# Early Strassen blocks: weight splits and conversion moved into second-layer steps, and two tiles of the last plain chunk put between the first block's halves

## The chip, the cores and the metric

The kernel runs as one program on one core of one Trainium2 chip. The metric is the device time of that core in microseconds (us). Most executions of a kernel agree within 0.3%.

## The reference, cut to what matters

Attention over 2 batches, 8 heads, 576 tokens of 64 values gives `x` (1152 tokens by 512). Two feed-forward stages follow:

```
p = domain_probs / (domain_probs.sum(-1, keepdims=True) + 1e-09)
for e in range(E):                       # E = 4, w1[e]: 512 x 1024, w2[e]: 1024 x 512
    h = np.maximum(x @ w1[e], 0.0)
    out += p[:, e:e + 1] * (h @ w2[e])
...
h = x @ w_in                             # 512 x 2048
g = h * (1.0 / (1.0 + np.exp(-1.702 * h)))
return (g @ w_out)                       # 2048 x 512
```

All of it is wanted in fp32. The kernel makes each fp32 product out of three products of rounded parts: every operand is split into a rounded part (`hi`, made by ScalarE) and the rest (`lo`, raw minus `hi`, made by VectorE), and hi*hi + lo*hi + hi*lo are added up in PSUM.

## The kernel before, in words

The hidden layers are cut into 12 blocks of 512 hidden units (8 of the first stage, numbers 0 to 7, and 4 of the second). A `visit` is one block with a list of chunks of tokens; its first layer (512 inputs to 512 hidden units) has one step per group `g` of 128 hidden units, and its second layer one step per tile of 128 tokens, 12 matrix products of 128x512 each (line 972). The first-layer weights of a visit are called "a", those of the second layer "b"; each comes as four pieces g = 0 to 3, loaded in pairs into four buffers `wst` by SyncE's queue, and each piece is split by `split_w`: ScalarE writes `whi` (line 60), and VectorE `wlo` (line 230) when `rest` is run, one step later.

Visits 0 to 6 are plain: their chunks run while attention is still going on. Visit 6 ends with chunk 3, tokens 768 to 1151, which is three tiles in its second layer. Visits 7, 8 and 9 (blocks 3, 1 and 0) are the first three that compute the first layer by Strassen's scheme over two chunks of 320 tokens; this text calls them **block 1, block 2 and block 3**, and visit 10 **block 4**. Each of blocks 1 to 3 has

- a first half and a second half (kind 3, 7 steps each, one product of 6 matrix instructions per step, line 885). In the listings a product is known by its operands: `xh` or `th` are tokens and sums of tokens, `whi` is a weight and `sh` a sum of weights. A half begins with xh,whi and ends with xh,sh, which adds the last product to the bank `pc`;
- the second layer (kind 4, 8 steps on five banks: the first five tiles with half of the hidden units, and then three of them with the other half), and
- two steps left over (kind 5), which run between the halves of the next block.

Around the products, each half has a chain of small work on the 320-column banks: ScalarE copies the bank of the first product to `u` (line 909); VectorE adds the second product to it (line 930), makes a second sum (line 914), and writes `jc` (line 891, three times), of which the first must have read the bank `pc` before the last product may be added there. ScalarE applies relu (line 893) and rounds to `hh`, GpSimd makes `hl` (line 895). The remaining quarter goes through lines 962 and 963.

The sums of weights are made by GpSimd (`sr`, lines 251 to 254) and split by `split_sums` into `sh` (ScalarE, two instructions) and `sl` (VectorE, line 267, two). There is one buffer each for `sh` and `sl`, so a half's sums are written after the half before has read its own. `evac_l2` (line 1005, or 1003 for the first visit of a tile) adds a finished tile of the second layer to the result.

Where the splits stand is written out by hand in `place()` for visits 7 to 9, and the order of the instructions of VectorE, ScalarE, GpSimd and TensorE in these visits is fixed as the code issues them (`pin_turn`). What is issued for visit 6 is not fixed so: the scheduler puts it where it likes. Each engine works through its own queue in order.

`mlp_convert` runs beside all this: the second stage's weights arrive as 8-byte numbers and each of 32 pieces is turned into fp32 by one ScalarE and six VectorE instructions (lines 342 to 357), one `yield` at a time; `cv_due` says how many per step. The pieces are stored to DRAM and loaded again into `wst` when their block comes.

Of the kernel before, what the change touches and what calls it, by code (L numbers as in the profile page):

```python
# [21 lines left out]
NCH = len(CH)  # L22
# [3 lines left out]
OVER = 2  # L26
# [8 lines left out]
NMOE = 8  # L35
# [4 lines left out]
def attn_moe_mlp(ctx: ExitStack, tc: tile.TileContext, qk0, qk1, qk2, v0, vp, fg, dp, wa_moe, wb_moe, wa_mlp, wb_mlp, out):  # L40
# [115 lines left out]
    for p_, u in zip(units[1:], units[2:]):  # L156
        seq += [(1,) + u, (2,) + p_]
    seq.append((2,) + units[-1])
    before = []
    for v_ in range(v_exp, len(visits)):  # L160
        b, cs = visits[v_]
        if v_ == v_mlp:
# [16 lines left out]
    w_turn = [("a", 0), ("b", 0)]  # L179
    for u in seq:  # L180
        if u[1] + 1 < len(visits) and u in (last_l1[u[1]], last_l2[u[1]]):
            w_turn.append(("ab"[u[0] in (2, 4, 5)], u[1] + 1))
    w_pairs = [(k, v_, g) for k, v_ in w_turn for g in (0, 2)]
    w_loaded = [0]
    w_owed = [0]
# [939 lines left out]
        return rest  # L1125

    def steps(kind, v_, b, c):
        return {1: 4, 2: len(tiles(c)), 3: 7, 4: 10 - OVER, 5: OVER}[kind]

    split_q = []  # L1130

# [12 lines left out]
    def place():  # L1144

        at = {}

        def put(u, g, what, *args):
            at.setdefault((u, g), []).append((what, args))

        for v_ in range(v_exp, v_all):
            b, (c1, c2) = visits[v_]
            h0, h1, l2 = (3, v_, b, c1), (3, v_, b, c2), (4, v_, b, c1)
            put(h0, 1, sum_weights, v_ + 1, 0)
            put(h1, 1, sum_weights, v_ + 1, 1)
            put(l2, 0, split_sums, v_ + 1, 0)
            put((5, v_, b, c1), 0, split_sums, v_ + 1, 1)
            first = v_ == v_exp
            places = [(h1, 1), (h1, 3), (l2, 1), (l2, 2)]
            for g, (u, i) in enumerate(places):  # L1160
                put(u, i, split_w, "a", v_ + 1, g)
            if first:
                for k, (u, i) in enumerate([(h0, 2), (h0, 4), (h1, 4), (h1, 6)]):
                    put(u, i, split_w, "b", v_, k)
            for k, i in enumerate((3, 4, 6, 7) if first else (3, 4, 5, 6)):
                put(l2, i, split_w, "b", v_ + 1, k)
        return at

    place_at = place()
    evac = [lambda: None]  # L1170
# [3 lines left out]
    for i, (kind, v_, b, c) in enumerate(seq):  # L1174
# [17 lines left out]
            j_gen = emit_joint(v_, b, m)  # L1192
        n_steps = steps(kind, v_, b, c)
        for g in range(n_steps):
            if kind in (2, 4, 5):
                split_until("b", v_, range(4))
            else:
                split_until("a", v_, [g] if kind == 1 else range(4))
            if i == 0:
                ev = lambda: None  # L1200
            elif kind == 3:
                ev = next(j_gen)
            else:
                ev = {1: emit_l1, 2: emit_l2, 4: emit_l2_joint}[kind](v_, b, c, g) if kind < 5 else emit_l2_joint(v_, b, c, g, True)
            for _ in range(sums_at.get(u, 0)):
                in_turn(next, ts_gen, None)
            if sum_due:
                sv, sm = sum_due[0][:2]
                if (sv, 0) in j_done if sm else sv - 1 not in joint or (sv - 1, 1) in j_done:
                    split_sums()  # L1210
            if kind == 3 and g == 6:
                j_done.add((v_, m))
            n = 0
            if nxt:
                j, cc = nxt[0]
                left = sum(steps(*u) for u in seq[i:j]) - g
                n = max(0, -(-(due[cc] - pulled[0]) // left))
                for _ in range(n):
                    pull()
            rests = []  # L1220
            for d in split_due[:]:
                d[0] -= 1
                if d[0] == 0:
                    split_due.remove(d)
                    rests.append(split_output(d[1]))
            evac[0]()
            for r in rests:
                r()
            evac[0] = ev
            split_next()  # L1230
            if len(split_q) > 4:
                split_next()
            for what, args in place_at.get((u, g), ()):
                what(*args)
            if v_ + 1 < len(visits) and not v_exp <= v_ < v_all:
                if u == last_l1[v_] and kind == 1:
                    split_q.append(("a", v_ + 1, g))
                elif u == last_l1[v_] and g in (3, 5):
                    split_q.append(("a", v_ + 1, g // 4))
                if u == last_l2[v_] and g == n_steps - 1 and v_ + 1 != v_exp:  # L1240
                    split_q.extend(("b", v_ + 1, k) for k in range(4))
            if late:

                if sums_at.get(u, 0) < 2:
                    cv_due[0] += (0.25 if v_ < v_all else 1.55 if b < NMOE else 1.3) * (4 / n_steps)
                while cv_due[0] >= 1:
                    in_turn(next, cv_gen[0], None)
                    cv_due[0] -= 1
                load_owed()
            if v_ >= v_exp:  # L1250
                (pin_engines.add if v_ < v_all else pin_engines.discard)(nc.tensor.engine)
                pin_turn()
            else:
                pin_from[1] = len(nc.cur_bb.bb.instructions)
# [58 lines left out]
```

## Time and profile before

| | |
|---|---|
| median of 3 runs | 708.8 us (706.63 to 709.87) |
| profiled execution: time | 709.05 us |
| its span, first to last instruction | 707.3 us |
| mean granted TensorE clock | 0.995 |
| busy share of the span | TensorE 97%, VectorE 72%, ScalarE 48%, GpSimd 32% |

The span is read against the time of its own execution, 1.75 us more. TensorE's share says that only some 19 us of the span can be won without taking work from it; where these lie is what the views below are for. In the timeline a row `x2` is two instructions merged, its start is the first's start, and `[1.61 <-ACT sh L60]` is the time that the engine stood idle before it and the instruction that ended the wait. The chain of work that ended last is followed back from the last instruction.

### The profile page before, as it was taken

How to read it: one execution, taken by the hardware profiler on the slowest of the kernel's cores; microseconds unless marked ns; L12 is line 12 of the kernel's file. 1: busy time of each engine (PE TensorE's matmuls, PEld its weight loads, DVE VectorE, ACT ScalarE, POOL GpSimd, SP SyncE). 2: the span in 40 equal slices, each digit the busy share in tenths (PEclk: the TensorE clock that was granted, in tenths of full speed). 3: DMA queues.
4: the chain of work that ended last, by engine and by line, in shares of the span. 5: the costliest groups of instructions: out<-in, count | busy, mean ns of one | idle time of the engine just before them, and what ended most of it. 6: DMA issues, size and time to landing. Idle time of an engine off the chain costs nothing.

```text
span 707.3 us, 10721 instructions
## 1 busy us (share of the span) xinstructions
PE 688.6 (97%) x3829; PEld 598.4 (85%) x3829; DVE 510.6 (72%) x1057; ACT 341.8 (48%) x789; POOL 225.0 (32%) x266
## 2 busy tenths in 40 slices
PE   8999999999999799899999999999999999999997
PEld 4797888888898687888888888887899898998986
DVE  6896766676386668685868977887888878675632
ACT  5777766676432734443443343335355455352430
POOL 6887566622223535411412314112102212000000
PEclk9999999999999899999999999999999999999999
DMA  7686744432310333232324424424320444120012
GB/s 266 225 283 234 268 146 159 126 100 82 118 31 31 90 90 109 84 134 86 98 101 150 145 94 136 155 92 144 115 104 31 130 138 150 60 76 0 1 45 89
DMA packets 38597, 83.37 MB, mean 118 GB/s; under 512 B 3560, under 2 KB 3568, under 8 KB 38544
## 3 DMA queue, kind: packets, MB, share of 16 engines
q1 hardware_dynamic: 38504, 82.65, 35.6%
q8 instruction: 30, 0.49, 0.3%
q14 instruction: 23, 0.19, 0.1%
q10 hardware_dynamic: 40, 0.04, 0.0%
HBM read 71.88 MB, written 10.78 MB: 117 GB/s over the span
## 4 chain that ended last, share of the span: by engine, by line
PE 81%; DVE 11%; ACT 3%; issue 2%; POOL 1%; DMA 1%; SPq 0%; DVEq 0%; POOLq 0%; ACTq 0%
PE m L972 36%; PE m L847 19%; PE m L885 14%; PE s L568 4%; PE x L672 4%; PE t L642 3%; DVE wlo L230 2%; DVE hl L963 1%; DVE acc L1005 1%; DVE sl L267 1%; DVE cvd L355 1%; DVE wf L357 1%; DVE jc L891 1%; ACT jc L893 1%; ACT hh L60 1%
## 5 line engine op out<-in xcount | busy, mean ns | idle before, releaser
L972 PE MATMUL m<-whi,hh 128*128 128x512 f32 x432 | 123.2, 395 | 0.2
L972 PE MATMUL m<-wlo,hh 128*128 128x512 f32 x432 | 119.9, 392 | 0.0
L972 PE MATMUL m<-whi,hl 128*128 128x512 f32 x432 | 119.3, 391 | 0.0
L230 DVE TENSOR_TENSOR wlo<-wst,whi 128x512 fp32r<-128x512 f32 x140 | 109.7, 800 | 5.3 <-ACT whi L60 4.7
L972 PEld LDWEIGHTS m<-wlo,hh 128*128 128x128 f32 x432 | 81.5, 189 | 17.3
L972 PEld LDWEIGHTS m<-whi,hl 128*128 128x128 f32 x432 | 81.2, 189 | 17.0
L895 POOL TENSOR_TENSOR hl<-jc,hh 128x320 fp32r<-128x320 f32 x42 | 37.4, 892 | 178.1 <-ACT hh L60 168.1
L60 ACT ACTIVATE whi<-wst 128x512 fp32r<-128x512 f32 x144 | 85.0, 625 | 15.7 <-DMA wst<-in_wa_moe_dram 7.0
L972 PEld LDWEIGHTS m<-whi,hh 128*128 128x128 f32 x432 | 79.7, 189 | 14.6 <-DVE acc L1005 0.8
L893 ACT ACTIVATE jc<-jc 128x320 f32<-128x320 f32 x42 | 19.7, 470 | 111.3 <-DVE jc L891 111.3
L251 POOL TENSOR_TENSOR sr<-wst 128x256 f32<-128x256 f32 x20 | 18.7, 936 | 147.1 <-DVE tl L287 49.1
L624 POOL TENSOR_SCALAR e<-e,sm 128x128 f32<-128x128 f32 (+4 forms) x72 | 47.6, 672 | 54.4 <-DVE sm L622 28.1
L847 PE MATMUL m<-xh,whi 128*128 128x256 f32 (+2 forms) x304 | 64.2, 328 | 0.0
L847 PE MATMUL m<-xh,wlo 128*128 128x256 f32 (+2 forms) x304 | 64.2, 325 | 0.0
L847 PE MATMUL m<-xl,whi 128*128 128x256 f32 (+2 forms) x304 | 63.8, 326 | 0.0
L963 DVE SCALAR_TENSOR_TENSOR hl<-m,hh 128x384 fp32r<-128x384 f32 (+2 forms) x82 | 36.0, 439 | 27.9 <-ACT hh L962 27.5
L1005 DVE SCALAR_TENSOR_TENSOR acc<-m,dpn,acc 128x512 f32<-128x512 f32 x63 | 46.8, 746 | 12.7 <-PE m L972 12.6
L847 PEld LDWEIGHTS m<-xh,whi 128*128 128x128 f32 x304 | 50.3, 189 | 3.7 <-DVE acc L1005 0.5
L847 PEld LDWEIGHTS m<-xh,wlo 128*128 128x128 f32 x304 | 50.6, 189 | 2.6
L847 PEld LDWEIGHTS m<-xl,whi 128*128 128x128 f32 x304 | 50.3, 189 | 2.8
L966 DVE TENSOR_TENSOR hl<-m,hh 128x384 fp32r<-128x384 f32 x48 | 26.7, 556 | 29.0 <-ACT hh L60 28.9
L614 ACT ACTIVATE e<-e,mx 128x128 f32<-128x128 f32 (+4 forms) x72 | 41.6, 580 | 11.7 <-DVE mx L598 11.2
(138 smaller groups left out, 1296.6 us busy)
## 6 DMA issues: line engine op xcount, KB each, us to landing
wst<-in_wa_moe_dram SPq DMA_DIRECT2D x28, 512.0 KB, 3.6
wst<-in_wb_moe_dram SPq DMA_DIRECT2D x28, 512.0 KB, 4.3
mst<-in_wa_mlp_dram SPq DMA_DIRECT2D x16, 512.0 KB, 3.8
wm<-wf SPq DMA_DIRECT2D x32, 256.0 KB, 3.3
mst<-in_wb_mlp_dram SPq DMA_DIRECT2D x16, 512.0 KB, 4.1
wst<-wm SPq DMA_DIRECT2D x16, 512.0 KB, 3.7
cb<-cumd SPq DMA_DIRECT2D x16, 256.0 KB, 3.9
qr<-in_qk_dram SPq DMA_DIRECT2D x8, 384.0 KB, 4.8
```

The source lines that it names most:

```text
L60: return nc.scalar.activation(out=out, in_=in_, func=AF.Copy)
L230: (nc.gpsimd if v_ == 0 and kind == 'a' and g < 4 else nc.vector).tensor_sub(lf, raw, f(hf))
L568: nc.tensor.matmul(pt[:, :z - a], lhsT=lr[i][0], rhs=lr[i][1], start=i == 0 and not (both and pt is not bank), stop=i == n - 1, skip_group ...
L614: nc.scalar.activation(out=e[:, off:off + w], in_=e[:, off:off + w], func=AF.Exp, scale=-1.0, bias=mx, accum_out=sm[:, 0, k:k + 1])
L624: nc.gpsimd.tensor_scalar(out=e[:, off:off + w], in0=e[:, off:off + w], scalar1=sm[:, 0, i:i + 1], scalar2=1.0, op0=ALU.mult, op1=ALU.mult)
L672: nc.tensor.matmul(pt[64 * g:64 * g + 64, o:n], lhsT=lhsT, rhs=rhs, start=i == 0, stop=i == nk - 1)
L847: nc.tensor.matmul(p[:, :n], lhsT=w[:, k, :], rhs=x[c][:, k, :], start=(j == 0 and k == 0), stop=(j == 2 and k == 3))
L885: nc.tensor.matmul(p[:, :WN], lhsT=w[a][:, k, :], rhs=x[z][:, k, :], start=start and j == 0 and k == 0, stop=stop and j == 2 and k == 1, s ...
L895: nc.gpsimd.tensor_sub(hl[:, g, :], r, f(hh[:, g, :]))
L963: nc.vector.scalar_tensor_tensor(out=l_, in0=q, scalar=0.0, in1=f(h_), op0=ALU.max, op1=ALU.subtract)
L972: nc.tensor.matmul(p, lhsT=h_tile(v_, b, c, j, x, k), rhs=wb[v_, k][w].rearrange("p a c -> p (a c)"), start=i == 0 and k == 0, stop=i == 2 ...
L1005: nc.vector.scalar_tensor_tensor(out=a, in0=p, scalar=d, in1=a, op0=ALU.mult, op1=ALU.add)
```

## The change

Four things, in one diff. (1) The second layer of visit 6's last chunk keeps one step; its last two tiles become a kind of their own, 6, issued between the halves of block 1, and the split of the sums for block 1's second half is put behind the first of them. (2) In blocks 1 to 3 the splits leave the early steps of the second half (steps 1 and 3; in block 1 also 2 and 4 of the first half and 4 of the second) for steps 5 and 6 of the second half and 1 to 6 of the second layer; block 1, which also splits its own "b", has two more at each end (steps 0 and 1 of its first half, and of block 2's). (3) The second layer no longer wants all of "b" split at its start; the rests are run when the half that needs them begins. (4) The conversion gets 0.75 of a step's share in the second-layer steps of blocks 1 to 3 and none in their products (0.25 in all before), and 1.4 in place of 1.55 later.

```diff
-    before = []
+    before = [(6,) + units[-1]]
...
-            w_turn.append(("ab"[u[0] in (2, 4, 5)], u[1] + 1))
+            w_turn.append(("ab"[u[0] not in (1, 3)], u[1] + 1))
...
     def steps(kind, v_, b, c):
-        return {1: 4, 2: len(tiles(c)), 3: 7, 4: 10 - OVER, 5: OVER}[kind]
+        if (kind, v_) == (2, v_exp - 1) and c == NCH - 1:
+            return len(tiles(c)) - OVER
+        return {1: 4, 2: len(tiles(c)), 3: 7, 4: 10 - OVER, 5: OVER, 6: OVER}[kind]
...
             first = v_ == v_exp
-            places = [(h1, 1), (h1, 3), (l2, 1), (l2, 2)]
-            for g, (u, i) in enumerate(places):
-                put(u, i, split_w, "a", v_ + 1, g)
+            places = [(h1, 5), (h1, 6)] + [(l2, i) for i in range(1, 7)]
             if first:
-                for k, (u, i) in enumerate([(h0, 2), (h0, 4), (h1, 4), (h1, 6)]):
-                    put(u, i, split_w, "b", v_, k)
-            for k, i in enumerate((3, 4, 6, 7) if first else (3, 4, 5, 6)):
-                put(l2, i, split_w, "b", v_ + 1, k)
+                put((6,) + units[-1], 0, split_sums_done)
+                nxt0 = (3, v_ + 1, visits[v_ + 1][0], c1)
+                places = [(h0, 0), (h0, 1)] + places + [(nxt0, 0), (nxt0, 1)]
+            todo = [("b", v_)] * first + [("a", v_ + 1), ("b", v_ + 1)]
+            for (kind, w_, g), (u, i) in zip([(*t, g) for t in todo for g in range(4)], places):
+                put(u, i, split_w, kind, w_, g)
         return at
+
+    def split_sums_done():
+        if sum_due:
+            sv, sm = sum_due[0][:2]
+            if (sv, 0) in j_done if sm else sv - 1 not in joint or (sv - 1, 1) in j_done:
+                split_sums()
...
-            if kind in (2, 4, 5):
+            if kind in (2, 6):
                 split_until("b", v_, range(4))
-            else:
+            elif kind not in (4, 5):
                 split_until("a", v_, [g] if kind == 1 else range(4))
...
-                ev = {1: emit_l1, 2: emit_l2, 4: emit_l2_joint}[kind](v_, b, c, g) if kind < 5 else emit_l2_joint(v_, b, c, g, True)
+                if kind in (4, 5) and ("b", v_, 2 if kind == 5 or g > 4 else 0) in lo_of:
+                    split_rest()
+                ev = (emit_l1(v_, b, c, g) if kind == 1 else emit_l2(v_, b, c, g) if kind == 2 else
+                      emit_l2(v_, b, c, g + len(tiles(c)) - OVER) if kind == 6 else emit_l2_joint(v_, b, c, g, kind == 5))
...
-                    cv_due[0] += (0.25 if v_ < v_all else 1.55 if b < NMOE else 1.3) * (4 / n_steps)
+                    cv_due[0] += ((0.75 if kind == 4 else 0) if v_ < v_all else 1.4 if b < NMOE else 1.3) * (4 / n_steps)
```

Both programs hold the same instructions on every engine; only their order differs. TensorE first, in the middle of block 1's first half after the change (line 972 is one of the two tiles of visit 6, line 885 a product; the last row is the half's last product's first pair):

```order
L885 MATMUL m<-tl,sh 128x320 x2
L972 MATMUL m<-whi,hh 128x512 x4
L972 MATMUL m<-wlo,hh 128x512 x4
L972 MATMUL m<-whi,hl 128x512 x4
L972 MATMUL m<-whi,hh 128x512
L885 MATMUL m<-th,sh 128x320 x2
...
L885 MATMUL m<-tl,whi 128x320 x2
L972 MATMUL m<-whi,hh 128x512
L972 MATMUL m<-wlo,hh 128x512 x4
L972 MATMUL m<-whi,hl 128x512 x4
L885 MATMUL m<-xh,sh 128x320 x2
```

Before, all six rows of line 972 stood ahead of the half. Now the scheduler has put them not behind the half but into it: one tile ahead of the fourth product, the rest of the other ahead of the last one.

VectorE next, from the end of block 1's first half to the sums of block 2 (line 267 the second time); before:

```order
L891 TENSOR_TENSOR jc<-u_3073,m 128x320
L267 TENSOR_TENSOR sl<-sr,sh 128x512 x2
L891 TENSOR_TENSOR jc<-m,u_3072 128x320
L343 TENSOR_SCALAR cvt<-cvt 128x512
L230 TENSOR_TENSOR wlo<-wst,whi 128x512
L930 TENSOR_TENSOR u_3168<-m,u_3168 128x320
L230 TENSOR_TENSOR wlo<-wst,whi 128x512
L914 TENSOR_TENSOR u_3169<-m,u_3168 128x320
L891 TENSOR_TENSOR jc<-m,u_3169 128x320
L891 TENSOR_TENSOR jc<-u_3169,m 128x320
L230 TENSOR_TENSOR wlo<-wst,whi 128x512
L963 SCALAR_TENSOR_TENSOR hl<-m,hh 128x320
```

and after the change:

```order
L891 TENSOR_TENSOR jc<-m,u_3047 128x320
L267 TENSOR_TENSOR sl<-sr,sh 128x512 x2
L930 TENSOR_TENSOR u_3163<-m,u_3163 128x320
L914 TENSOR_TENSOR u_3164<-m,u_3163 128x320
L891 TENSOR_TENSOR jc<-m,u_3164 128x320
L891 TENSOR_TENSOR jc<-u_3164,m 128x320
L963 SCALAR_TENSOR_TENSOR hl<-m,hh 128x320
L230 TENSOR_TENSOR wlo<-wst,whi 128x512
L891 TENSOR_TENSOR jc<-m,u_3163 128x320
L230 TENSOR_TENSOR wlo<-wst,whi 128x512
L267 TENSOR_TENSOR sl<-sr,sh 128x512 x2
```

No `wlo` and no conversion stands between the sums and the first `jc` of the second half any more, and the last `jc` of the first half stands ahead of the sums.

VectorE again, after the change, from block 1's second layer into block 2's first half (lines 930 and 914 are block 2's):

```order
L346 TENSOR_SCALAR cvt<-cvt 128x512
L1005 SCALAR_TENSOR_TENSOR acc_79<-m,dpn,acc_79 128x512
L230 TENSOR_TENSOR wlo<-wst,whi 128x512
L1005 SCALAR_TENSOR_TENSOR acc_2863<-m,dpn,acc_2863 128x512
L230 TENSOR_TENSOR wlo<-wst,whi 128x512
L349 SCALAR_TENSOR_TENSOR wf<-mst,cvt 128x512
L1005 SCALAR_TENSOR_TENSOR acc_2863<-m,dpn,acc_2863 128x512
L230 TENSOR_TENSOR wlo<-wst,whi 128x512
L930 TENSOR_TENSOR u_3348<-m,u_3348 128x320
L230 TENSOR_TENSOR wlo<-wst,whi 128x512
L914 TENSOR_TENSOR u_3349<-m,u_3348 128x320
```

Before, the two rows of line 230 around line 930 were not there: the last `wlo` stood ahead of the last line 1005, and a single conversion between that and line 930.

## Rows read from the trace of the kernel before

**Rows 1.** The page: span, and busy time with share and count of instructions.
```profile
span 707.3 us, 10721 instructions
...
PE 688.6 (97%) x3829; PEld 598.4 (85%) x3829; DVE 510.6 (72%) x1057; ACT 341.8 (48%) x789; POOL 225.0 (32%) x266
```

**Rows 2.** Windows: stretch, its length, busy us of each engine, granted clock, DMA.
```profile
221.28:252.99 31.71, 26.92 (x134) 23.48 (x132) 20.28 (x32) 15.82 (x33) 13.69 (x14) 0.89 0.27 84
252.99:281.52 28.53, 26.49 (x146) 23.58 (x145) 20.33 (x32) 13.78 (x29) 13.58 (x14) 1.00 0.27 81
281.52:310.05 28.53, 26.49 (x146) 23.58 (x144) 20.76 (x37) 13.21 (x28) 9.11 (x10) 1.00 0.28 81
310.05:341.00 30.95, 30.95 (x167) 27.69 (x166) 20.31 (x39) 11.85 (x27) 9.21 (x11) 1.00 0.34 107
```

**Rows 3.** Waits of PE over the span: total us, times, longest.
```profile
PE m L885 <- DVE jc L891: 5.8, 3, 2.5
```

**Rows 4.** The chain of work that ended last: start, us, engine, tile, instructions.
```profile
240.43 12.72 PE m L972 x48
...
253.15 6.17 PE m L885 x42
...
270.77 10.91 PE m L972 x48
```

**Rows 5.** Timeline, PE, block 1: start, us, operation; idle before and its releaser.
```profile
230.97 0.55 PE L885 MATMUL m<-th,sh 128*128 128x320 f32 x2 [1.61 <-ACT sh L60]
...
231.94 0.56 PE L885 MATMUL m<-th,sl 128*128 128x320 f32 x2 [0.42 <-DVE sl L267]
...
234.83 0.56 PE L885 MATMUL m<-xh,whi 128*128 128x320 f32 x2 [0.28 <-ACT u L909]
...
238.46 0.90 PE L885 MATMUL m<-xh,sh 128*128 128x320 f32 x2 [2.49 <-DVE jc L891]
```

**Rows 6.** Timeline, ScalarE and VectorE, second half of block 1.
```profile
234.35 0.42 ACT L909 ACTIVATE u<-m 128x320 f32<-128x320 f32 x1
...
236.60 0.81 DVE L230 TENSOR_TENSOR wlo<-wst,whi 128x512 fp32r<-128x512 f32 x1
...
237.91 0.49 DVE L891 TENSOR_TENSOR jc<-m,u 128x320 f32<-128x320 f32 x1
```

**Rows 7.** Timeline, VectorE and PE, second half of block 2.
```profile
263.94 0.42 DVE L352 TENSOR_SCALAR cvt<-wf 128x512 uint32<-128x512 uint32 x1
...
265.07 0.56 PE L885 MATMUL m<-th,sh 128*128 128x320 f32 x2 [0.39 <-DVE acc L1005]
...
266.20 1.23 DVE L230 TENSOR_TENSOR wlo<-wst,whi 128x512 fp32r<-128x512 f32 x1
...
268.50 0.48 DVE L914 TENSOR_TENSOR u<-m,u 128x320 f32<-128x320 f32 x1
...
269.63 0.56 PE L885 MATMUL m<-xh,sh 128*128 128x320 f32 x2 [1.65 <-DVE jc L891]
```

**Rows 8.** Timeline, VectorE and GpSimd, second layers of blocks 2 and 3.
```profile
275.89 1.12 POOL L251 TENSOR_TENSOR sr<-wst 128x256 f32<-128x256 f32 x1 [1.23 <-DVE sl L267]
...
276.33 4.67 DVE L230 TENSOR_TENSOR wlo<-wst,whi 128x512 fp32r<-128x512 f32 x4
...
285.23 0.49 DVE L914 TENSOR_TENSOR u<-m,u 128x320 f32<-128x320 f32 x1 [0.32 <-PE m L885]
...
304.60 2.48 DVE L230 TENSOR_TENSOR wlo<-wst,whi 128x512 fp32r<-128x512 f32 x4
```

**Rows 9.** Timeline, VectorE, the last two blocks.
```profile
640.60 0.69 DVE L1011 TENSOR_TENSOR acc<-m,acc 128x512 f32<-128x512 f32 x1
...
664.63 0.68 DVE L230 TENSOR_TENSOR wlo<-wst,whi 128x512 fp32r<-128x512 f32 x1
```

**Rows 10.** The page's DMA issues: tile, queue, count, KB each, us to landing.
```profile
wm<-wf SPq DMA_DIRECT2D x32, 256.0 KB, 3.3
...
wst<-wm SPq DMA_DIRECT2D x16, 512.0 KB, 3.7
```

More of the change, by code (lines that the diff above doesn't have):

```diff
@@ L1203, in attn_moe_mlp @@
             else:
-                ev = {1: emit_l1, 2: emit_l2, 4: emit_l2_joint}[kind](v_, b, c, g) if kind < 5 else emit_l2_joint(v_, b, c, g, True)
+                if kind in (4, 5) and ("b", v_, 2 if kind == 5 or g > 4 else 0) in lo_of:
+                    split_rest()
+                ev = (emit_l1(v_, b, c, g) if kind == 1 else emit_l2(v_, b, c, g) if kind == 2 else
+                      emit_l2(v_, b, c, g + len(tiles(c)) - OVER) if kind == 6 else emit_l2_joint(v_, b, c, g, kind == 5))
             for _ in range(sums_at.get(u, 0)):
                 in_turn(next, ts_gen, None)
[L1207 to L1210, printed above, removed]
+            if sum_due and kind != 6:
+                split_sums_done()
             if kind == 3 and g == 6:
```

## Prediction, made before the changed kernel had run

> **What bounds the kernel now.** I read the page first: TensorE is busy for 688.6 of 707.3 us [rows 1], so the change can only win back idle or slow TensorE time; it takes no work away. Next, windows, cut at the first product of blocks 1 to 4 [rows 2]. TensorE idles 4.8 us in block 1 (31.71 less 26.92) and 2.0 us each in blocks 2 and 3, and block 1 also runs at a granted clock of 0.89. Block 4 has no idle time at all. So the stretch to look at is 221.28 to 310.05, 88.8 us.
>
> What would it take without waits? The chain of work shows it [rows 4]: the two halves run 6.17 us each where nothing stops them (42 instructions), a second layer 10.91 us (48), so a tile, 12 instructions, is 2.73 us. Block 1 holds 6.17 + 6.17 + 10.91 = 23.25 us, blocks 2 and 3 with two left-over steps 2.73 more, 25.98. Against the windows, **8.46 us are lost in block 1 and 2.55 in each of the others: 13.56 in all**. That is more than the idle time: after the waits block 1's second layer took 12.72 us in place of 10.91 [rows 4], the same 48 instructions at the lower of the clock's two levels (1.2 for 2.4 GHz) for part of it, and the product ahead of it was slowed too.
>
> Where the losses stand, the timeline says [rows 5]: four waits in block 1's second half, 1.61 + 0.42 us for the sums, 0.28 for `u`, and 2.49 for the first `jc`, 4.8 together. Blocks 2 and 3 have the same two places each: 0.39 us for a bank that line 1005 empties, and 1.65 for the first `jc` [rows 7]; over the span the first `jc` costs 5.8 us in three waits [rows 3]. It is a chain, second sum, `jc`, last product, and the queues of VectorE and ScalarE are in order. In block 1, ScalarE copies `u` only at 234.35 and a `wlo` of 0.81 stands ahead of the second sum [rows 6]; in block 2 two `wlo` and a conversion lie between the bank and the second sum, which starts at 268.50 [rows 7], although the product it adds, the second from 265.07 on, should have ended near 267.0 (two products of 0.88, a seventh of 6.17 each, and an estimated 0.2 of drain).
>
> **The change, part by part.**
>
> *Two tiles inside the first half.* TensorE's work is moved, not made: 2 x 2.73 us that stood ahead of block 1 now stand in its first half. That half's chain (its last `jc` above all) had no filler; the second tile, about 2.0 us of it, now runs ahead of the last product, while VectorE and ScalarE finish the other outputs. The sums may be written when the last product has read the old ones. Before, ScalarE was then still behind with the outputs of the half, and its `sh` released TensorE only at 230.97; now its queue is nearly empty by then, and TensorE has two products (1.76 us) to run before it needs `sh`. I take the first two waits as gone, 2.0 us. If the queue is as late as before, they stay: that is a rival.
>
> *Splits and conversion out of the second halves.* Ahead of the first `jc`, block 1 loses two `wlo`, one conversion and the ScalarE instructions that fed them; blocks 2 and 3 two `wlo` and two conversions (0.42 us the one at 263.94). What is left is a floor: from second sum to last product took 1.13 us in block 2 (268.50 to 269.63), the second sum must wait for the fourth product's end, some 0.2 us of drain, and TensorE has one product, 0.88, to run meanwhile. So 0.45 us stay in each block, 1.35 in all. For the bank, the conversion at 263.94 no longer stands ahead of line 1005; of 0.39 us I keep 0.2, twice: 0.4.
>
> *What it adds: a fuller VectorE in the second layer.* Nothing waits there, five banks are under way, but the next block's first half has its own second sum, and the work put in front of it must be done by then. Before, in block 3, VectorE reached it 0.32 us early [rows 8], and TensorE can bear 0.65 more (two products, 1.76, against 1.13). After the change, block 2's second layer has two `wlo` more in front of the sums (they fill waits for ScalarE, but push the sums back by at most 1.24 us, two times the 0.62 below; I take 1.1) and one conversion more (0.42 is the row of one, a `wlo` is 0.62; I take 0.6): 1.7 against 0.97, a wait of some 0.7 to 0.9 us; I take 0.9 for block 3. In block 1's second layer eight `wlo` follow the sums in place of six, the last two of them on either side of line 930. The price of one is bounded by two rows: 2.48 us for four where GpSimd rests, 0.62 each, and 4.67 for four, 1.17 each, beside GpSimd's sums of weights (about 1.1 us each) [rows 8]. GpSimd's four sums for block 3 come when the weights' load has landed, late in block 1's second layer, so three or four instructions of VectorE stand against them. All at the low price: VectorE is on time, no wait. All four sums against `wlo`: 2.2 us late, a wait of 2.1. The likely place is between, nearer to the high one since the load cannot be earlier: 1.2 us for block 2. Together 2.1 us, with bounds of 0 and 3.9.
>
> The Trainium skill, "SBUF — State Buffer", section "Who interferes with whom", says that a VectorE instruction with two SBUF inputs and a GpSimd instruction that reads SBUF exclude each other for the whole instruction. The 1.17 us per `wlo` beside GpSimd agree with it; by that rule each `wlo` there costs a whole GpSimd instruction, and the whole would come to 701.8 us.
>
> *Conversions later in the program.* Blocks 1 to 3 do 9 yields for 12, and the rate of 1.4 for 1.55 makes 12 fewer in blocks 4 to 7, so the last piece is finished between two instructions of line 1011 near 640.6 [rows 9]. Its store and load land in 3.3 and 3.7 us [rows 10], by 648; the first split of that pair's block is at 664.63. Nothing waits. The loads of weights in blocks 1 to 3 move by a few us with the splits that free their buffers; the landing is still ahead of the split that needs it, and of GpSimd's sums only the time changes.
>
> *The clock.* In block 1 it fell after 4.8 us of waits within 8 us; in block 2 waits of 0.39 and 1.65, 4 us apart, left it at 1.00 [rows 2, 7]. The waits I leave are of the second kind. So block 1's 1.81 us in the second layer come back, and what the slowed product ahead of it lost: of the 8.46, the waits (4.80) and the 1.81 leave 1.85; blocks 2 and 3 lose 2.55 with waits of 2.04, some 0.25 beyond each wait, so 1.0 for four, and 0.85 is the product's. Together 2.7.
>
> *Sum.* Lost before 13.56; left 1.35 + 0.4 + 2.1 = 3.85, and some 0.1 us of refill at each of seven waits, 0.7: 4.55. Gain 9.0 us against the profiled execution's own time: 709.05 - 9.0 = **700.0 us**. That execution is 0.25 us above the median of the runs shown, which is no more than their scatter. With VectorE on time it would be 697.9, with the high bound 701.8; its own range is 697.5 to 702.5.
>
> **Rivals.**
>
> *The filler doesn't cover the sums.* The two tiles stand inside the half and not behind it, so between its last product and the sums of the second there are still only two products. If ScalarE is late as before, the waits of 2.0 us stay, with 0.25 beyond each, and with 0.45 more at the `jc` the clock may fall again for 2.7: 5.2 back, **705.2 us**. For it: the order. Against: the queue that made ScalarE late has lost its split and its wait for the first output.
>
> *VectorE becomes the bound at the starts of blocks 2 and 3.* At the high bound in both, 1.8 us more than the sum, with the clock falling after each for 2.7 us as it did in block 1: 700.0 + 1.8 + 5.4 = **707.2 us**, no change. For it: VectorE had only 0.32 us in hand [rows 8]. Against: the single 1.65 us of block 2 left the clock up.
>
> *Slower.* The same place, one mechanism, VectorE's backlog: to end above 712.6 us the two starts must wait 12.6 us more than I forecast, 6.3 each. Eight `wlo` at 1.17 in place of 0.62 would make 4.4 us, so it needs a backlog that is carried from one block into the next. VectorE is busy for 20.3 of 28.5 us in a block [rows 2], and its work doesn't grow, so it should drain.
>
> **How the numbers follow.** What can be told from no change here is 0.5%, 3.5 us: faster is below 705.5, slower above 712.6. Forecast as summed 0.62, better than its range 0.03, the first rival with what lies between it and the sum 0.19, the second 0.12, slower 0.04. Faster 0.84, same 0.12, slower 0.04. The range reaches from 697.5 to 704.5: it leaves out 0.03 below and some 0.17 above.
>
> **What would show it.** Right: the four waits of block 1's second half shrink to one of about 0.45 us before the last product; granted clock 1.00 there; the second layer of block 1 takes 10.9 us; waits of 0.5 to 2 us before the last product of the first halves of blocks 2 and 3, released by `jc`, where there were none; blocks 1 to 3 with the two tiles take about 85 us in place of 94; no new wait after block 4 starts. Wrong: `sh` still releasing TensorE for over a microsecond in block 1, a granted clock below 1.00 in any of the three blocks, a first half of block 2 or 3 with a wait above 2.5 us, or waits for `whi` or `wst` late in the program.

## The result, and the profile after

The changed kernel takes 697.6 us (median of 3 runs, 696.63 to 697.74) where the kernel before takes 708.8: a ratio of 0.984, 95% interval 0.980 to 0.988. The profiled execution took 696.63 us. The forecast was 700.0 with a range from 697.5 to 704.5: the time lies just inside its lower end. The execution of the kernel before whose trace is used here (709.05 us) was a long one: of 29 later executions 6 have its mean granted clock of 0.995 and a median of 709.5 us, and the other 23, at 0.997 to 1.000, one of 707.0, so about 2 us of every gain that is counted below against that trace go with the fall of the clock in it.

The page of the changed kernel, as [rows 1]:

```profile
span 694.9 us, 10725 instructions
...
PE 683.6 (98%) x3828; PEld 596.3 (86%) x3829; DVE 502.1 (72%) x1057; ACT 342.1 (49%) x789; POOL 221.2 (32%) x266
```

Windows of it, cut at the first products of blocks 1 to 4 as in [rows 2] (block 1 now holds the two tiles):

```profile
216.20:245.46 29.26, 28.96 (x157) 25.81 (x156) 20.21 (x35) 15.85 (x33) 11.00 (x13) 1.00 0.16 49
245.46:272.59 27.13, 26.49 (x146) 23.57 (x144) 19.15 (x33) 13.62 (x29) 15.62 (x17) 1.00 0.31 103
272.59:299.88 27.29, 26.61 (x145) 23.60 (x144) 19.20 (x35) 13.67 (x29) 9.75 (x12) 1.00 0.32 106
```

Block 1 with its two tiles has 23.25 + 5.46 = 28.71 us of work, so 0.55 us is lost there; blocks 2 and 3, with 25.98 each, lose 1.15 and 1.31. That is 3.0 us for 13.56 before, and the granted clock is 1.00 in all three. The chain has the second layer of block 1 at its full speed, and the first halves of blocks 2 and 3 nearly without a wait (before: [rows 4]):

```profile
234.73 10.90 PE m L972 x48
245.62 6.15 PE m L885 x42
...
272.75 6.26 PE m L885 x42
```

TensorE's waits in blocks 1 to 3, from its timeline; [rows 5, 7] are those of before:

```profile
233.58 0.56 PE L885 MATMUL m<-xh,sh 128*128 128x320 f32 x2 [0.30 <-DVE jc L891]
...
257.50 0.56 PE L885 MATMUL m<-th,sh 128*128 128x320 f32 x2 [0.34 <-DVE acc L1005]
...
260.70 0.56 PE L885 MATMUL m<-xh,sh 128*128 128x320 f32 x2 [0.30 <-DVE jc L891]
...
284.76 0.57 PE L885 MATMUL m<-th,sh 128*128 128x320 f32 x2 [0.38 <-DVE acc L1005]
...
287.97 0.57 PE L885 MATMUL m<-xh,sh 128*128 128x320 f32 x2 [0.30 <-DVE jc L891]
```

The two waits for sums are gone, the three for the first `jc` are 0.30 us each in place of 2.49, 1.65 and 1.65, and the two bank waits are as they were. Where the forecast had 2.1 us of waits, at the starts of blocks 2 and 3, there is none: VectorE's queue is full up to the second sum but arrives in time. Its timeline there, at the start of block 2, with GpSimd's:

```profile
246.46 0.68 DVE L349 SCALAR_TENSOR_TENSOR wf<-mst,cvt 128x512 uint32<-128x512 uint32 x1
...
246.56 1.19 POOL L251 TENSOR_TENSOR sr<-wst 128x256 f32<-128x256 f32 x1 [6.82 <-DVE wlo L230]
...
247.06 0.74 DVE L1005 SCALAR_TENSOR_TENSOR acc<-m,dpn,acc 128x512 f32<-128x512 f32 x1
...
247.71 1.30 POOL L252 TENSOR_TENSOR sr<-wst 128x256 f32<-128x256 f32 x1
...
247.73 0.68 DVE L230 TENSOR_TENSOR wlo<-wst,whi 128x512 fp32r<-128x512 f32 x1
...
248.73 0.83 DVE L230 TENSOR_TENSOR wlo<-wst,whi 128x512 fp32r<-128x512 f32 x1
...
249.48 0.48 DVE L914 TENSOR_TENSOR u<-m,u 128x320 f32<-128x320 f32 x1
```

Three of GpSimd's sums stand against this stretch, as forecast, but it is GpSimd that waits (1.19 and 1.30 us, where such a sum takes 0.74 alone), and one `wlo` alone is longer, 0.83 for 0.68.

One thing was not forecast. Counting TensorE's matrix instructions one by one, the changed kernel is 10.5 us ahead at the end of block 3's second layer, counted from the last plain second layer ahead of block 1, and another 2.2 us ahead at the end of the program: 3.2 us are won in blocks 5 to 7 and 1.0 lost in the last four. (It is 0.4 us behind at the point that this is counted from, up to which the two programs have the same work; the profiled executions below lie between 0.2 us ahead and 1.7 us behind there.)

### The profile page after: what moved, and what is told of

The parts are those of the page before. It is cut to its first block, busy times and chain, and to the rows that moved or that the text cites. A ratio compares the mean times of both kernels' runs of the same rounds, so it can differ in the third digit from the quotient of the medians.

```text
span 694.9 us, 10725 instructions
## 1 busy us (share of the span) xinstructions
PE 683.6 (98%) x3828; PEld 596.3 (86%) x3829; DVE 502.1 (72%) x1057; ACT 342.1 (49%) x789; POOL 221.2 (32%) x266
## 4 chain that ended last, share of the span: by engine, by line
PE 93%; DVE 3%; POOL 1%; ACT 1%; issue 1%; DMA 1%; SPq 0%; POOLq 0%; DVEq 0%; ACTq 0%
PE m L972 42%; PE m L847 20%; PE m L885 17%; PE s L568 4%; PE x L672 4%; PE t L642 3%; PE m L1117 1%; DMA dpraw<-in_dp_dram 1%; POOL ks L494 0%; PE m L864 0%; POOL e L624 0%; PE t L716 0%; PE m L1033 0%; POOL qlo L512 0%; PE s L571 0%
## 5 line engine op out<-in xcount | busy, mean ns | idle before, releaser
L230 DVE TENSOR_TENSOR wlo<-wst,whi 128x512 fp32r<-128x512 f32 x140 | 103.0, 751 | 4.9 <-ACT whi L60 4.3
L624 POOL TENSOR_SCALAR e<-e,sm 128x128 f32<-128x128 f32 (+4 forms) x72 | 46.0, 651 | 54.5 <-DVE sm L622 27.5
```

The lines of the kernel that those rows point to most:

```text
L230: (nc.gpsimd if v_ == 0 and kind == 'a' and g < 4 else nc.vector).tensor_sub(lf, raw, f(hf))
L624: nc.gpsimd.tensor_scalar(out=e[:, off:off + w], in0=e[:, off:off + w], scalar1=sm[:, 0, i:i + 1], scalar2=1.0, op0=ALU.mult, op1=ALU.mult)
```

## The experiments

My theory after the result: each part of the change takes away the waits at its own place, the new rate of the conversion wins the 2.2 us behind block 4, and VectorE's queue ahead of the second sums of blocks 2 and 3 has no room left. Rivals: one part does it all; the late gain is a matter of phase; VectorE has room. In the table all ratios are to the kernel before on the same chip; the last two columns are the us by which TensorE gets ahead of the kernel before up to the end of block 3's second layer, and behind it, counted as above in the profiled executions.

| kernel | median us | ratio, 95% interval | won in blocks 1 to 3 | behind them |
|---|---|---|---|---|
| changed kernel again (e0) | 697.08 | 0.9857 [0.9834, 0.9881] | 10.0 | 2.3 |
| tiles only (e1) | 702.66 | 0.9929 [0.9913, 0.9944] | 5.0 | 1.8 |
| places only (e2) | 702.46 | 0.9925 [0.9908, 0.9943] | 7.3 | 0.1 |
| rate only (e3) | 703.21 | 0.9937 [0.9921, 0.9953] | 4.2 | 2.3 |
| all but the rate (e4) | 698.10 | 0.9869 [0.9850, 0.9888] | 9.5 | 1.7 |
| 4 VectorE instructions more, twice (e5) | 702.67 | 0.9935 [0.9913, 0.9958] | 4.1 | 2.3 |
| products swapped (e6) | 695.16 | 0.9826 [0.9802, 0.9850] | 11.9 | 2.3 |
| bank first (e7) | 695.98 | 0.9837 [0.9813, 0.9861] | 11.3 | 2.3 |
| GpSimd's sums later (e9) | 697.18 | 0.9854 [0.9833, 0.9875] | 10.1 | 2.3 |
| late rate 1.6 (e11) | 700.24 | 0.9898 [0.9877, 0.9920] | 10.0 | -0.4 |
| swap, bank, late rate (e8) | 697.18 | 0.9852 [0.9826, 0.9878] | 12.9 | -0.4 |
| the same, GpSimd's sums later (e10) | 697.44 | 0.9860 [0.9838, 0.9882] | 13.1 | -0.4 |

**The parts one by one.** e1 against the changed kernel, the places of before put back and the rate (and, not shown, the second layer wants all of "b" split at its start again):

```diff
-            places = [(h1, 5), (h1, 6)] + [(l2, i) for i in range(1, 7)]
+            places = [(h1, 1), (h1, 3), (l2, 1), (l2, 2)]
...
-                    cv_due[0] += ((0.75 if kind == 4 else 0) if v_ < v_all else 1.4 if b < NMOE else 1.3) * (4 / n_steps)
+                    cv_due[0] += (0.25 if v_ < v_all else 1.55 if b < NMOE else 1.3) * (4 / n_steps)
```

> The changed kernel with only the two tiles between the halves of block 1 and the earlier place of the split of the sums; the splits of the weights and the conversion stand where they stood before. My theory (each part takes away the waits at its own place): in block 1's second half the two waits for the sums (1.61 and 0.42 us) are gone, a wait for the first jc stays, like the 1.65 us of block 2 or somewhat more, since a split and a conversion still stand ahead of it; the clock stays at 1.00, so that the second layer of block 1 takes 10.9 us and not 12.7; blocks 2 and 3 keep their 0.39 and 1.65 us; about 702.5 us (4.8 of the 8.46 us lost in block 1, and 1.5 us of scatter either way). Rival (the places and not the tiles do it): the waits for the sums stay because the queues of ScalarE and VectorE are as late as before, the clock falls again, and the time is 706 us or more.

e2, against the changed kernel, so that parts (2) and (3) of the change are left:

```diff
-    before = [(6,) + units[-1]]
+    before = []
...
-                put((6,) + units[-1], 0, split_sums_done)
```

and the old rates; e3 is the kernel before with the changed line of the rates, e4 the changed kernel with the old one.

> The changed kernel without the two tiles between the halves (they stand ahead of block 1 again) and with the old rates of the conversion: the new places of the splits alone. My theory: the waits for the sums in block 1's second half stay at 1.5 to 2.0 us together, since the first half ends as late for ScalarE as before; the waits for the first jc shrink to 0.5 to 0.9 us in blocks 1 to 3, where the conversion that is still there may add its 0.4; with waits of 2.5 to 3 us in block 1 in place of 4.8 the clock is left at 1.00, and the time is 701 to 703 us; if the clock still falls, 704. Rival (the tiles do nearly all in block 1): block 1 still loses more than 6 us of its 8.46 and the time is 705 us or more.

> The kernel before with the new rates of the conversion alone. Theory that the 2.9 us won behind block 4 come of the rate: the short stalls of TensorE between 370 and 501 us are gone, here too; one of about 0.7 us appears near 630 us; in blocks 1 to 3 the jc waits lose up to the 0.4 us of a conversion each; about 705 us, between 704 and 706. Rival (those 2.9 us come of where block 4 starts, so of the phase between the loads and the work, and not of the rate): behind block 4 the time is as before, and the whole is 707 to 708 us.

> The changed kernel with the old rates of the conversion alone. Theory that the rate gives what was won behind block 4: the 2.9 us between blocks 5 and 7 are lost again, the 1.0 us near 619 us comes back, and in blocks 1 to 3, where conversions stand in the second halves again, the first jc is 0.4 to 0.8 us later in each; about 700.5 to 701.5 us. Rival (the rate does nothing): 697 to 698 us.

TensorE's waits, from the timelines: e1,

```profile
234.94 0.55 PE L885 MATMUL m<-xh,sh 128*128 128x320 f32 x2 [1.38 <-DVE jc L891]
253.23 0.56 PE L885 MATMUL m<-xh,sh 128*128 128x320 f32 x2 [0.97 <-DVE jc L891]
260.72 0.56 PE L885 MATMUL m<-th,sh 128*128 128x320 f32 x2 [0.97 <-DVE acc L1005]
```

e2,

```profile
231.23 0.56 PE L885 MATMUL m<-th,sh 128*128 128x320 f32 x2 [0.48 <-ACT sh L60]
232.20 0.56 PE L885 MATMUL m<-th,sl 128*128 128x320 f32 x2 [0.42 <-DVE sl L267]
...
237.04 0.57 PE L885 MATMUL m<-xh,sh 128*128 128x320 f32 x2 [0.81 <-DVE jc L891]
```

and e3:

```profile
238.27 0.64 PE L885 MATMUL m<-xh,sh 128*128 128x320 f32 x2 [2.22 <-DVE jc L891]
267.05 0.55 PE L885 MATMUL m<-xh,sh 128*128 128x320 f32 x2 [0.65 <-DVE jc L891]
```

The two tiles alone take both waits for sums away and leave a `jc` wait of 1.38 us; the clock stays at 1.00. So the rival that the filler doesn't cover the sums fell. The new places alone shorten the same waits too, 1.61 us to 0.48, and 0.90 us for both where I had expected 1.5 to 2.0: the two splits that moved from steps 2 and 4 of block 1's first half to its first two steps were, it seems, part of why ScalarE was late. That it was these two was not tried by itself. The gains in blocks 1 to 3 are 5.0, 7.3 and 4.2, 16.5 together, for 10.0 to 10.5 of the whole: the parts overlap, since either of the first two is enough to keep the clock up (1.00 in both; with the rate alone the second layer of block 1 still takes 11.94 us). By the medians, with the late gain in them, the three win 13.6 us together for 10.3. They also get in each other's way: e1 loses 0.97 us at block 2's start and 0.97 for a bank, where before there was no wait and one of 0.39.

In e3 the `jc` wait of block 2 went from 1.65 to 0.65 us, where I had expected up to 0.4 us less. Two conversions, not one, have left its second half (0.42 and 0.68 us), and the `wlo` that stood behind them takes 0.82 us for 1.23.

Behind block 4, the rate alone is enough for the whole 2.3 us; but e4, with the old rate, still has 1.7 of it (so it takes 698.1 us where I had expected 700.5 to 701.5), and e2, with the same rate, 0.1. So the rival is half right: it matters on which steps the pieces of the conversion fall, and the two steps of the moved tiles, which count their share of the conversion like any others, shift that too. What the short stalls were is shown for one place in the kernel before, its timeline near the end of block 7:

```profile
493.11 0.66 PE L1117 MATMUL m<-identr,acc 128*128 128x128 f32 x4 [0.59 <-DVE acc L1005]
...
491.97 0.42 DVE L352 TENSOR_SCALAR cvt<-wf 128x512 uint32<-128x512 uint32 x1
492.31 0.74 DVE L1005 SCALAR_TENSOR_TENSOR acc<-m,dpn,acc 128x512 f32<-128x512 f32 x1
...
493.57 1.23 DVE L355 SCALAR_TENSOR_TENSOR cvd<-mst,cvt 128x512 f32<-128x512 uint32 x1
494.83 1.11 DVE L357 TENSOR_TENSOR wf<-wf,cvd 128x512 f32<-128x512 f32 x1
495.87 0.74 DVE L1005 SCALAR_TENSOR_TENSOR acc<-m,dpn,acc 128x512 f32<-128x512 f32 x1
```

TensorE's transposes (line 1117) wait 0.59 us for the first eviction, right ahead of which stands a conversion; two more lie between it and the second, for which the next transposes start at 496.66. The chain of waits of the kernel before runs through VectorE and ScalarE from 477.95 to 496.62 us. In the changed kernel the same two evictions start at 478.78 and 481.11 us, 1.30 and 2.19 us ahead of their transposes (0.80 and 0.79 before), and TensorE doesn't wait.

**The room in VectorE's queue, and the price beside GpSimd.** e5 adds, after the last step of the second layers of blocks 1 and 2,

```diff
+        x = f(ts[0][0][:, 0, :240])
+        for _ in range(4):
+            nc.vector.tensor_sub(late["dx"].tile([128, 240], F32, tag="dx", name="dx"), x, x)
```

> The changed kernel itself once more, to stand on the same chip beside the three others of this group. Theory that its gain is 11 us or so: 0.984 of the kernel before, within 0.003. Rival (part of the gain was the chance of the first comparison): 0.987 or more, where it would not differ from the changed kernel with the old rates of the conversion (0.9869).

> The changed kernel with four more subtractions of 128x240 on VectorE at the end of the second layers of blocks 1 and 2, about 0.3 us each by an estimate from the 0.68 us of 128x512, so 1.2 us; their result is not used. Theory (the VectorE queue is full from the second layer up to the second sum of blocks 2 and 3, and its room of about 4.15 us after the block's start is just used up): a wait of 1.0 to 1.3 us for the first jc ahead of the last product of the first halves of blocks 2 and 3, where there is none; about 2.3 us more than the changed kernel. Rival (VectorE still has a microsecond in hand there): no wait and no more than 0.3 us.

Its timelines, TensorE and VectorE (its lines are numbered one higher: 886 for 885, 892 for 891, 973 for 972), and behind them a row of TensorE in e0:

```profile
253.38 0.56 PE L886 MATMUL m<-xh,sh 128*128 128x320 f32 x2 [3.02 <-DVE jc L892]
...
283.81 0.57 PE L886 MATMUL m<-xh,sh 128*128 128x320 f32 x2 [2.04 <-DVE jc L892]
...
245.93 3.00 DVE L1178 TENSOR_TENSOR dx<-th 128x240 f32<-128x240 f32 x4
248.84 1.23 DVE L349 SCALAR_TENSOR_TENSOR wf<-mst,cvt 128x512 uint32<-128x512 uint32 x1
...
279.17 1.73 DVE L1178 TENSOR_TENSOR dx<-th 128x240 f32<-128x240 f32 x4
...
278.38 0.55 PE L885 MATMUL m<-xh,sh 128*128 128x320 f32 x2 [0.40 <-DVE jc L891]
```

The dose was larger than I had estimated, 1.7 us where GpSimd rests and 3.0 beside its sums, and the conversion behind it took 1.23 us for 0.68. TensorE's waits answer it nearly one for one: 3.02 us where there was none, and 2.04 where the changed kernel's second run had 0.40. There is no room in that queue; the rival fell. The wait of 3.02 also took the clock along, the one of 2.04 didn't. The chain and the windows of e5:

```profile
254.53 4.34 PE m L973 x12
```

```profile
254.00:258.00 4.00, 4.00 (x14) 3.19 (x13) 1.29 (x4) 2.98 (x8) 2.21 (x3) 0.60 0.32 123
```

A tile of 2.75 us took 4.34. The three together, 3.0 + 1.6 + 1.6, are what e5 lost in blocks 1 to 3 against e0 (5.9), less a bank wait of 0.35 that went.

e9 moves GpSimd's sums away from that queue:

```diff
-            put(h0, 1, sum_weights, v_ + 1, 0)
+            put(h0, 5, sum_weights, v_ + 1, 0)
```

> The changed kernel with GpSimd's sums of weights for the next block's first half issued four steps later, so that they run after the second sum of blocks 2 and 3 and not beside the second layer ahead of it. Theory (VectorE and GpSimd take turns there, each instruction of one holding up one of the other: 1.22 us for 0.68 on VectorE twice ahead of block 3, 0.83 for 0.68 once ahead of block 2): none of VectorE's instructions ahead of the second sum is longer than 0.75 us, block 3's second sum is 1.1 us earlier against the block's start and the wait of 0 to 0.4 us before its first half's last product is gone, GpSimd's sums take 0.74 us each; 0 to 0.6 us less than the changed kernel. Rival (VectorE's long instructions come of something else, the loads for example): they stay at 1.2 us, and the time is the same; or the later sums are late for sh, and TensorE waits for it.

Its timeline, VectorE ahead of block 3's second sum, and at the sums of block 2, with GpSimd's row beside:

```profile
268.78 1.88 DVE L230 TENSOR_TENSOR wlo<-wst,whi 128x512 fp32r<-128x512 f32 x3
270.59 0.68 DVE L355 SCALAR_TENSOR_TENSOR cvd<-mst,cvt 128x512 f32<-128x512 uint32 x1
...
276.22 0.49 DVE L914 TENSOR_TENSOR u<-m,u 128x320 f32<-128x320 f32 x1 [0.77 <-PE m L885]
...
254.65 2.04 DVE L267 TENSOR_TENSOR sl<-sr,sh 128x512 fp32r<-128x512 f32 x2 [2.03 <-ACT sh L60]
...
254.82 2.60 POOL L895 TENSOR_TENSOR hl<-jc,hh 128x320 fp32r<-128x320 f32 x2
```

The same two rows of the changed kernel:

```profile
268.87 2.43 DVE L230 TENSOR_TENSOR wlo<-wst,whi 128x512 fp32r<-128x512 f32 x3
...
271.22 1.22 DVE L355 SCALAR_TENSOR_TENSOR cvd<-mst,cvt 128x512 f32<-128x512 uint32 x1
```

So the contention is shown: with GpSimd away, the three `wlo` take 1.88 for 2.43 us and the conversion 0.68 for 1.22, and VectorE stands idle 0.77 us before the second sum. It gained nothing in time: GpSimd's other work is pushed back too, meets the `sl`, which take 2.04 for 1.55 us, and the bank waits behind them grew from 0.34 and 0.38 to 0.70 and 0.54 (697.18 us, for 697.08 in e0).

**The two waits that were left.** e6 puts, in the second halves of blocks 1 to 3, the product of the second sum ahead of the one that fills `pc`:

```diff
+                product(pd[0], s3, ts[3], True, True)
+                yield lambda: nc.vector.tensor_add(u[1], pd[0][:, :WN], u[0])
+                product(pc, s1, ts[1], True, True)
```

> The changed kernel with two products of the second halves of blocks 1 to 3 in the other order: the one whose sum is the second sum (line 914) comes ahead of the one that fills the bank pc, so that only the first jc stands between the fourth product and the last. Theory (the 0.30 us of idle time left before each last product are the floor of the chain second sum, jc, product, one step of which now lies beside a product): the three waits vanish, and the time is 1.0 to 1.4 us below the changed kernel. Rival (the wait then goes over to the bank or the second half of the sums, which the moved product needs one product earlier): the same time, with a wait of 0.3 to 0.5 us at that product in place of it.

e7:

```diff
-            put((5, v_, b, c1), 0, split_sums, v_ + 1, 1)
+            put((5, v_, b, c1), 1, split_sums, v_ + 1, 1)
```

> The changed kernel with the split of the second half's sums put one left-over step later, so that the first eviction of line 1005 stands ahead of the two sl of line 267 on VectorE and not behind them. Theory (the 0.34 and 0.38 us that blocks 2 and 3 wait for a bank are a matter of this order: VectorE idles 2 us there for sh, with the eviction ready): both waits are gone, 0.7 to 1.0 us below the changed kernel. Rival (the eviction pushes sl back, and TensorE waits for sl instead): within 0.3 us of the changed kernel, with waits for sl in blocks 2 and 3.

Both do what their theories say. In e6 the three `jc` waits of the second halves and one of the two bank waits are gone; in e7 both bank waits are, since VectorE now evicts while it would wait for `sh`, as its timeline shows:

```profile
253.16 0.75 DVE L1005 SCALAR_TENSOR_TENSOR acc<-m,dpn,acc 128x512 f32<-128x512 f32 x1
255.20 1.56 DVE L267 TENSOR_TENSOR sl<-sr,sh 128x512 fp32r<-128x512 f32 x2 [1.29 <-ACT sh L60]
```

What the bank wait of a second half is made of can be read from the runs above. The first column is the start of line 914 in the first half, counted from the block's first product; the conversion is the one that stands on VectorE ahead of the eviction of line 1005:

| second sum of the first half, us | conversion ahead of the eviction, us | wait for the bank, us | where |
|---|---|---|---|
| 3.72 | none | under 0.1 | e3, block 2 |
| 3.71 | 0.42, 0.41 | 0.39 | kernel before, blocks 2 and 3 |
| 3.71 | 0.68 | 0.65 | e1 and e4, block 3 |
| 4.02, 4.14 | none | 0.34, 0.38 | changed kernel, blocks 2 and 3 |
| 4.51 | 0.41 | 0.70 | e2, block 2 |
| 4.26, 5.27 | 0.68 | 0.96, 0.97 | e4 and e1, block 2 |

The first row's lines, VectorE and TensorE:

```profile
255.47 0.49 DVE L914 TENSOR_TENSOR u<-m,u 128x320 f32<-128x320 f32 x1 [0.51 <-PE m L885]
...
263.50 0.56 PE L885 MATMUL m<-th,sh 128*128 128x320 f32 x2
```

So two things add up. A conversion ahead of the eviction costs about its own length; and where the second sum of the first half is late, the split of the sums starts about 0.88 us into the second half in place of 0.58 (e0 and the kernel before), which costs the other 0.3. The change took the first away and brought the second; e7 moves the eviction out of the way of both.

Against e0 on the same chip e6 is 1.9 us faster (694.92 to 695.94 for 696.52 to 699.51) and e7 1.1 (695.85 to 696.42). Each beats the changed kernel's runs there; against the kernel before, the intervals of the three overlap.

**The late wait, and all together.** e11 sets the rate of the last four blocks to 1.6 in place of 1.3. e8 has the edits of e6, e7 and e11; e10 adds that of e9 to e8 ("the kernel before" in its expectation is e8).

> The changed kernel with the conversion's rate in the last four blocks at 1.6 in place of 1.3. Theory (the 0.68 us that TensorE waits near 620 us are a conversion, line 346, ahead of the jc of the last product but one on VectorE): the conversion is done before that place, the wait is gone, 1.0 us less than the changed kernel. Rival (VectorE is late there anyway): the same time, or new waits between 500 and 610 us.

> The changed kernel with three edits: the two products in the other order, the split of the second half's sums one step later, and the conversion's rate in the last four blocks at 1.6. If what they win adds up (floors of 0.30 idle and 0.1 beyond, three times; bank waits of 0.34 and 0.38; 1.0 near 620 us): 2.5 to 3 us below the changed kernel, about 694 us. Rival (the first two take away the same wait, since the swap alone already left one bank wait of two): 1.7 to 2 us below it.

> The three edits of the kernel before together with GpSimd's sums issued four steps later. If the last wait of 0.40 us before the last product of block 3's first half comes of the contention, this has no wait of TensorE of 0.3 us or more left in blocks 1 to 3: 0.3 to 0.5 us below the kernel with three edits, about 693.5 us. Rival: the same as it.

The theory of e11 fell. The changed kernel's timeline near 620 us,

```profile
618.33 0.42 DVE L346 TENSOR_SCALAR cvt<-cvt 128x512 uint32<-128x512 uint32 x1
618.66 0.56 DVE L891 TENSOR_TENSOR m<-u,m 128x384 f32<-128x384 f32 x1
...
620.30 0.50 PE L972 MATMUL m<-whi,hh 128*128 128x512 f32 x1 [0.68 <-ACT hh L60]
```

and that of e11:

```profile
573.96 0.50 PE L972 MATMUL m<-whi,hh 128*128 128x512 f32 x1 [0.62 <-ACT hh L60]
...
606.62 1.31 PE L885 MATMUL m<-th,sh 128*128 128x384 f32 x6 [0.78 <-ACT sh L60]
...
612.78 0.97 PE L847 MATMUL m<-xh,whi 128*128 128x384 f32 x4 [0.38 <-DVE acc L1011]
...
624.23 0.49 PE L972 MATMUL m<-whi,hh 128*128 128x512 f32 x1 [0.41 <-ACT hh L60]
```

With the denser conversion one wait became four, and 2.7 us are lost behind block 4 (2.3 won, then -0.4); which of its pieces stand ahead of what in these four was not followed up. That also spoils e8 and e10, for which I had expected about 694 and 693.5 us. Their gains in blocks 1 to 3 do add up: 12.9 and 13.1 us of the 13.56 that were lost. In e10 TensorE has no wait of 0.3 us or more left in these blocks. The first two edits with the rate of 1.3 were not run together, and neither was e10 with it. The fastest kernel measured is e6.

## Why the prediction was right, by its own steps

*Lost before, 13.56 us in blocks 1 to 3.* Held: e10 gets 13.1 us of it back.

*The sums' waits gone, 2.0 us.* Right, and by the mechanism given; the moved splits do part of it by themselves.

*The floor, 0.45 us three times.* Right: 0.30 us of idle time each, and 0.75 from one product's last pair to the next product's (259.95 to 260.70 us) where 0.29 is the pace, so 0.46 lost. e6 shows what it is made of: with the second sum beside a product, it is gone.

*The bank, 0.2 us twice.* Too small: 0.34 and 0.38. The conversion that I took for the cause was it: block 2 of e3, without one, has no such wait. But the wait came back from VectorE's late second sum (4.02 and 4.14 us after the block's start for 3.71), a price of its backlog that I had looked for at the last product alone. Start to start the two cost about 1.05 us, for 0.4 and 0.2 of refill in the sum.

*Refill, 0.1 us at each of seven waits.* Five waits were left, at 0.16 us each (0.46 less 0.30). The prediction reads 0.25 beyond each wait of before in one place and takes 0.1 in its sum; neither is the figure.

*VectorE's backlog, 1.2 + 0.9 us.* This is the term that was mis-sized most: at the place that the prediction names about 0.1 us was measured (0.4 at the start of block 3 in the second run of the same kernel, and 0.39 to 0.40 in e6, e7, e8 and e11); the rest of its price are the two bank waits. That the queue would be full was right, e5 shows it; the price was wrong. I counted three or four instructions of VectorE at the dear row, 1.17 for 0.62 us each, but in front of block 2 only one paid, 0.15 us. In front of block 3 three `wlo` and a conversion did pay, 1.09 us together; but before the change four `wlo` had paid 2.19 there (4.67 for 2.48), which the forecast did not take off, and the second sum is 0.75 us later than VectorE could have made it before, not 1.7. The dear row has four `wlo` back to back, each of which finds GpSimd in its way; in front of block 2 evictions and first sums, which read one operand from the banks, stand between, and GpSimd was the one to wait. The Trainium skill, "SBUF — State Buffer", section "Who interferes with whom", says that a VectorE instruction with at most one SBUF input, outside the two-port modes, doesn't contend, and that it is the order of issue that decides who blocks. I had used only its sentence on blocking. The 0.74 us of line 1005 beside GpSimd's 1.19 agree with the first; the second can't be told here, where GpSimd's 1.30 us start 0.02 us ahead of the `wlo` that they wait for.

*The clock, 2.7 us.* Right for the execution that was read: 1.00 in all three blocks, and the second layer of block 1 at 10.90 us. It is not what the change wins in every execution: the medians of e0 and of the kernel before on the same chip differ by 10.3 us, where the executions with the traces (697.08 and 709.05 us) differ by 12.0.

*Conversions later, "nothing waits".* Wrong by a term I had not looked for: I checked that the pieces would be ready in time, not which instructions they stand in front of. 2.2 us of the gain come from there, and e2, e4 and e11 show that this could as well have gone the other way. In the sum: 9.0 forecast for blocks 1 to 3, 10.0 to 10.5 measured, and 2.2 more.

The mechanism held where most of the gain was forecast, in block 1. That the time lies in the range owes something to luck: the two misses, the backlog's price and the late gain, go the same way, the median is 0.1 us above the range's lower end, and that of e0, 697.08 us, is below it.

What stays open: why the old rate wins 1.7 us behind block 4 with the moved tiles and 0.1 without them is argued from the count of steps, not tried by itself; and why the clock falls in some executions of the kernel before and less in others.

## What to carry to other kernels

Before a sum is built on one trace, compare its time with those of other executions. Before a wait is priced by a contended row, look at what stands between: instructions that contend back to back pay each, those with others between may let the other engine pay. Filler work that is spread over an in-order queue has no neutral place, so check not only when its result is wanted but what it stands in front of, and try several densities before trusting one. Where an engine waits for one input while another job of its queue is ready, put the ready one first.

## What the runs showed of the hardware that was not expected

A single wait of 3.02 us was followed by a granted clock of 0.60 over the stretch from 254 to 258 us (e5), a mean of the two levels of 1.2 and 2.4 GHz in which the lower has the larger part, while one of 2.04 us in the same kernel, and 1.38 and 0.97 us apart by 18 us in e1, left it at 1.00. Moving GpSimd's work out of VectorE's way did not remove the contention but moved it: ahead of block 3's second sum the three `wlo` took 0.55 us less and the conversion 0.54, and the two `sl` of block 2 took 0.49 us more (e9).
